# Moving a square root from ScalarE to VectorE at the entry of an attention backward pass, with spaced stores of q and a projection by whole tiles

## The chip, the cores and the metric

One core of one Trainium2 chip. The metric is the time of one execution on the device in microseconds (us). Two programs are compared by their fast runs of the same rounds on the same chip; "the span" is what a profile of one execution shows from its first to its last instruction, some 2 us less than its time.

## The reference

The program computes the output and all gradients of two attentions over the same tokens, in bf16. Part A is a linear attention and ends before the parts that matter here; part B is a softmax attention with 16 query heads and one head for k and v:

```python
def _B_ref(x, wq, wk, wv, wo):          # x: 1 x 2048 x 448
    B, S, D = x.shape
    H = 16
    Dh = D // H                          # 28, padded to 32 in the kernel
    q = (x @ wq).reshape(B, S, H, Dh).transpose(0, 2, 1, 3)
    k = x @ wk
    v = x @ wv
    scores = jnp.einsum("bhqd,bkd->bhqk", q, k) * (Dh ** -0.5)
    p = softmax(scores, axis=-1)
    o = jnp.einsum("bhqk,bkd->bhqd", p, v)
    return o.transpose(0, 2, 1, 3).reshape(B, S, H * Dh) @ wo
# out = concat([a, b]); outputs: out and the vjp of out for all eight inputs
```

## The kernel before: the parts that the change touches

The kernel first runs part A and the gradients that need no softmax (some 190 us), then the entry of part B, then a core of 512 units that computes exponentials, their transposes (eN, by DMA) and the products for dq, dk, dv and o, then a tail of some 75 us. The softmax needs no maximum: each row of q gets a shift, the root of |q|² times the largest |k|², written into a spare row of q.

The entry. Four quarters of q (512 tokens each) are projected; each gives its shift, a 16x512 tile; after two quarters the half of q is transposed by DMA into the tile qn and stored to qn_d in DRAM.

```python
        for qc in range(NQC):                      # four quarters of q
            ...                                    # projection, squares, sums of squares into pn
            shift = shifts[qc]
            nc.scalar.activation(out=shift, in_=pn[0:H, :], func=ACT.Sqrt, scale=kmax2[:, 0:1])
            for g in range(4):
                nc.gpsimd.dma_start(qT[:, g, qs].rearrange("(j r) s -> j r s", r=32)[:, 0, :], shift[4 * g:4 * g + 4, :])
            if qc % 2:
                q2 = slice((qc - 1) * 512, (qc + 1) * 512)
                t2 = slice(4 * qc - 4, 4 * qc + 4)
                for g in range(4):
                    nc.sync.dma_start_transpose(qn[:, t2, g * P:(g + 1) * P], qT[:, g, q2])
                nc.sync.dma_start(qn_d[q2, :].rearrange("(t p) c -> p t c", p=P), qn[:, t2, :])
```

Here qn is gaB, a tile that shows as gaT in the profile. The core, from its first exponential on:

```python
        do_slots = {u: divmod(n, 2) for n, u in enumerate([*range(1, 16), *range(17, 27, 2), *range(32, 128, 8)])}
        with tc.manual_schedule():
            tc.keep_in_program_order(nc.scalar.activation(out=ex[:], in_=ex[:], func=ACT.Exp))   # loads the table of exp
            for u in range(NU + 28):
                ...
                dpj = do_slots.pop(u, None)        # half a token tile of do = grad_out @ wo^T
                if dpj is not None:
                    dps_ = DB[u % 2] if u < 16 else dk_acc if u < 27 else spare
                    do_proj(*dpj, dps_)
                if hasS:
                    nc.scalar.activation(out=eT(u)[:, 0, :], in_=sp[0][:, :], func=ACT.Exp, scale=scale)
                ...
                # loads of q by tokens, for dk: four pieces per 256 tokens
                for a in {10: (0,), 14: (2,), 18: (1,), 22: (3,)}.get(u, ()) or {34: (0,), 42: (2,), 50: (1,), 58: (3,)}.get(u % 64, ()) * (u < 448):
                    ...
                    nc.gpsimd.dma_start(qX[qc][32 * a:32 * a + 32, :, :, :]..., qn_d[qc * 256:(qc + 1) * 256, :]...)
```

## Time and profile before

| kernel before | |
|---|---|
| time, median of 3 runs | 1078.06 us (1077.77 to 1078.93) |
| span of the profiled execution | 1079.1 us (its time: 1080.88 us) |
| first exponential of the core | 220.51 us |
| core, units 0 to 127 | 202.4 us |
| core, unit 128 to the last exponential | 581.3 us |
| tail | 75.0 us |

The prediction below walks through the views. In them PE is TensorE and PEld its weight loads, DVE is VectorE, ACT ScalarE, POOL GpSimd, SPq the queue of SyncE; a line of a timeline gives start and length in us, engine, line of the kernel, operation, result<-operands, shapes, count, and in brackets how long the engine idled before and what ended that (the releaser). An eviction is the copy of a result out of PSUM. Here is the head of the page alone: busy time of each engine, and the clock of TensorE in 40 slices of 27 us, in tenths of full speed. The one dip, an 8 in the tenth slice (243 to 270 us), lies in units 16 to 31 of part B's core.

```profile
PE 1027.6 (95%) x16326; PEld 489.1 (45%) x16329; DVE 895.5 (83%) x1792; ACT 876.7 (81%) x1744; POOL 772.1 (72%) x1014
...
PEclk9999999998999999999999999999999999999999
```

To compare executions I count the entry from "k0", the last eviction that ScalarE does for the gradients ahead of part B's entry (191.3 us here):

```profile
191.25 0.54 ACT L516 ACTIVATE wdq<-agen 128x448 bf16<-128x448 f32 x1 [1.54 <-PE agen L81]
192.17 0.69 ACT L563 ACTIVATE R<-agen,neg 128x512 bf16<-128x512 f32 x1 [0.37 <-PE agen L81]
```

The first eviction of k (the second line) follows 0.9 us later. The expectations below call k0 "the first eviction of k" or "the first row of k"; their numbers are counted from the first line.

### The profile page before, as it was taken

Reading aid. Unit: us, or ns where it says so; the run is one execution under the profiler, and the core shown is the slowest. Engines: PE = TensorE matmul, PEld = TensorE weight load, DVE = VectorE, ACT = ScalarE, POOL = GpSimd, SP = SyncE. Lnnn points to the kernel's source line nnn. Section 1 sums busy time; section 2 is a strip of 40 time slices with the busy share of each in tenths; the row PEclk is TensorE's granted clock in tenths of the full one; section 3 lists DMA queues with packets and bytes.
Section 4 is the critical chain, followed back from the end, with each engine's and each line's share of the span. In section 5 each row is a group of like instructions: output and inputs, shape, how many; then the busy total and the mean of one; then the engine's idle time right before and its main releaser. Section 6 shows DMA issues by size and latency. Waiting matters only on the chain.

```text
span 1079.1 us, 40135 instructions
## 1 busy us (share of the span) xinstructions
PE 1027.6 (95%) x16326; PEld 489.1 (45%) x16329; DVE 895.5 (83%) x1792; ACT 876.7 (81%) x1744; POOL 772.1 (72%) x1014
## 2 busy tenths in 40 slices
PE   9999999998999999999999999999999999999998
PEld 5555455443444444444444444444444444444434
DVE  7897400447999999999999999999999999999943
ACT  6463122577999999999999999999999999999622
POOL 6001243327888888888988888988998899888881
PEclk9999999998999999999999999999999999999999
DMA  9979899499999999999999999999999999999973
GB/s 239 165 131 195 161 196 193 88 215 169 202 210 198 179 190 187 197 188 201 183 187 191 201 188 194 204 184 182 193 203 186 193 194 193 196 177 180 221 140 92
DMA packets 669026, 199.36 MB, mean 185 GB/s; under 512 B 646008, under 2 KB 664736, under 8 KB 668840
## 3 DMA queue, kind: packets, MB, share of 16 engines
q1 hardware_dynamic: 656296, 175.23, 95.5%
q0 software_dynamic: 7584, 17.59, 6.9%
q10 hardware_dynamic: 4960, 3.96, 1.4%
q8 instruction: 128, 2.10, 0.8%
q14 instruction: 58, 0.48, 0.2%
HBM read 20.99 MB, written 12.94 MB: 31 GB/s over the span
## 4 chain that ended last, share of the span: by engine, by line
PE 34%; POOL 18%; ACT 18%; DVE 14%; issue 12%; DMA 4%; DVEq 0%; ACTq 0%; POOLq 0%; SPq 0%
POOL dsT L912 13%; PE agen L81 13%; ACT cp L911 9%; ACT eT L944 7%; DVE dsx L975 6%; PE sps L653 5%; PE aacc L81 4%; PE oq L653 4%; DVE dsT L909 3%; DMA eN<-eT 2%; PE dv_acc L653 2%; POOL prod L800 1%; PE dps L653 1%; DMA out_dram<-dsT 1%; DVE R L929 1%
## 5 line engine op out<-in xcount | busy, mean ns | idle before, releaser
L912 POOL TENSOR_TENSOR dsT<-cp,eT 128x512 bf16<-128x512 bf16 x512 | 588.4, 1157 | 104.5 <-ACT cp L911 98.6
L975 DVE STREAM_TRANSPOSE dsx<-dsT 128x512 f32<-128x512 f32 x512 | 357.7, 699 | 2.3 <-DVE R L723 0.2
L653 PEld LDWEIGHTS <-R 128*32 128x32 bf16 (+1 forms) x9184 | 229.5, 94 | 278.8 <-issue 238.7
L909 DVE TENSOR_TENSOR dsT<-dps,eT 128x512 bf16<-128x512 f32 x512 | 341.6, 667 | 16.5 <-PE dps L653 11.7
L904 ACT ACTIVATE eT<-sps 128x512 bf16<-128x512 f32 x512 | 312.6, 611 | 22.9 <-PE dps L653 10.7
L911 ACT ACTIVATE cp<-dps 128x512 bf16<-128x512 f32 x512 | 314.2, 614 | 12.0 <-PE dps L653 10.9
L944 ACT ACTIVATE eT<-sps 128x512 bf16<-128x512 f32 x512 | 320.3, 626 | 0.0
L653 PE MATMUL dk_acc<-dsx,qX 32*32 32x512 bf16 x4096 | 268.3, 376 | 0.0
L653 PE MATMUL dps<-doT,R 32*128 32x256 bf16 x2048 | 248.7, 270 | 1.9 <-ACT cp L911 0.8
L653 PE MATMUL sps<-R,R 32*128 32x256 bf16 (+1 forms) x2240 | 222.1, 274 | 7.6 <-DVE R L879 1.7
L653 PE MATMUL oq<-eT,R 128*32 128x256 bf16 x2048 | 158.3, 275 | 1.4 <-issue 1.4
L653 PE MATMUL oq<-dsT,R 128*32 128x256 bf16 x2048 | 157.1, 275 | 0.1
L653 PEld LDWEIGHTS <-qX 32*32 32x32 bf16 x4096 | 79.8, 89 | 114.4 <-issue 54.1
L653 PE MATMUL dv_acc<-eN,don 128*32 128x512 bf16 x1024 | 98.1, 381 | 3.8 <-DMA eN<-eT 3.8
L81 PEld LDWEIGHTS <-R 128*128 128x128 bf16 (+1 forms) x525 | 41.5, 98 | 41.7 <-issue 12.2
L406 POOL COPY pk<-R 128x256 bf16<-128x256 bf16 x4 | 1.6, 399 | 73.2 <-DVE R L366 73.1
L653 PEld LDWEIGHTS <-don 128*32 128x32 bf16 x1024 | 33.8, 97 | 5.0 <-issue 4.5
L422 DVE TENSOR_TENSOR osb<-aacc,pr 64x448 bf16<-64x448 f32 x2 | 1.2, 616 | 41.1 <-ACT pr L421 24.9
L800 POOL TENSOR_TENSOR prod<-R,oTs 128x128 f32<-128x128 bf16 x64 | 28.0, 438 | 7.7 <-DVE oTs L796 7.4
L929 DVE TENSOR_SCALAR R<-oq 64x256 bf16<-64x256 f32 x64 | 27.3, 427 | 3.6 <-PE oq L653 1.6
L817 PE MATMUL sps<-identB,don 128*32 128x128 bf16 x256 | 18.6, 224 | 12.3 <-POOL don L809 8.4
L81 PE MATMUL agen<-R,R 128*128 128x448 bf16 x128 | 28.6, 352 | 0.0
(232 smaller groups left out, 978.7 us busy)
## 6 DMA issues: line engine op xcount, KB each, us to landing
qX<-qn_d POOLq DMA_DIRECT2D x32, 256.0 KB, 4.3
out_dram<-osb ACTq DMA_DIRECT2D x22, 112.0 KB
qn_d<-gaT SPq DMA_DIRECT2D x2, 1024.0 KB
eN<-eT SPq DMA_TRANSPOSE x128
xa<-in_A_x_dram SPq DMA_DIRECT2D x8, 224.0 KB
ga<-in_grad_out_dram SPq DMA_DIRECT2D x4, 448.0 KB
xa<-in_grad_out_dram POOLq DMA_DIRECT2D x4, 448.0 KB, 12.2
out_dram<-wdq POOLq DMA_DIRECT2D x8, 224.0 KB, 6.3
```

Of the source, the lines that this page charges most:

```text
L81: nc.tensor.matmul(out_ap, lhsT=lhsT, rhs=rhs, start=start, stop=stop, tile_position=(0, 0))
L406: nc.gpsimd.tensor_copy(out=pk[:, t4, D:512], in_=gqn[:, t4, 3 * P:D])
L653: nc.tensor.matmul(out, lhsT=lhsT, rhs=rhs, start=start, stop=stop, tile_position=pos, skip_group_check=True)
L800: nc.gpsimd.tensor_tensor(out=prod[b][:], in0=dnv, in1=os_, op=ALU.mult)
L817: nc.tensor.transpose(tp2[q:q + 32, qb * P:(qb + 1) * P], don[b][:, qb, h, :], identB[:, :], tile_position=(0, q))
L904: nc.scalar.activation(out=eT(u)[:, 0, :], in_=sp[0][:, :], func=ACT.Exp, scale=scale)
L909: nc.vector.tensor_tensor(out=dst[:, 0, :], in0=dp[0][:, :], in1=ew[:, 0, :], op=ALU.mult)
L911: nc.scalar.activation(out=cp[:, :], in_=dp[1][:, :], func=ACT.Copy)
L912: nc.gpsimd.tensor_tensor(out=dst[:, 1, :], in0=cp[:, :], in1=ew[:, 1, :], op=ALU.mult)
L929: nc.vector.tensor_scalar(out=qT_B[g][64 * hp:64 * hp + 64, qc * 256:(qc + 1) * 256], in0=oq[64:128, 0:256], scalar1=scale, scalar2=None, ...
L944: nc.scalar.activation(out=eT(u)[:, 1, :], in_=sp[1][:, :], func=ACT.Exp, scale=scale)
L975: nc.vector.transpose(out=dsx[b][:, tp, :, :, :].rearrange("p h t c -> p (h t c)").bitcast(F32), in_=dsT[y][:, :, :].rearrange("p h c -> p ...
```

## The change

Its intent is to have no table loads on ScalarE for the square root, to take the second half's store off the entry, and to project do in fewer and larger pieces. Cut to its core:

```diff
-        return xbT, wq_pad, rep, bsel, gaB, ga[:, 8:12, :]
+        return xbT, wq_pad, rep, bsel, xa[:, 0:8, :], ga[:, 8:12, :], [flat(gaB[:, 2 * i:2 * i + 2, :]).bitcast(F32) for i in range(3)]
...
-            shift = shifts[qc]
-            nc.scalar.activation(out=shift, in_=pn[0:H, :], func=ACT.Sqrt, scale=kmax2[:, 0:1])
...
-            if qc % 2:
...
-                    nc.sync.dma_start_transpose(qn[:, t2, g * P:(g + 1) * P], qT[:, g, q2])
-                nc.sync.dma_start(qn_d[q2, :].rearrange("(t p) c -> p t c", p=P), qn[:, t2, :])
+            if qc == NQC - 1:
+                break
+            q_shift(pn, shifts[qc], qs, tmp)
+            if qc == 1:
+                for g in range(4):
+                    nc.sync.dma_start_transpose(qn[:, :, g * P:(g + 1) * P], qT[:, g, 0:1024])
+                nc.sync.dma_start(qn_d[0:1024, :].rearrange("(t p) c -> p t c", p=P), qn)
...
+    def q_shift(pn, shift, qs, tmp):
+        a, y, r = (t[0:H, :] for t in tmp)
+        nc.scalar.activation(out=a, in_=pn[0:H, :], func=ACT.Identity, bias=eps[:, 0:1], scale=kmax2[:, 0:1])
+        nc.vector.tensor_scalar(out=y.bitcast(mybir.dt.int32), in0=a.bitcast(mybir.dt.int32), scalar1=1, scalar2=None,
+                                op0=ALU.logical_shift_right)
+        nc.vector.tensor_scalar(out=y, in0=y, scalar1=0.485 * 2.0 ** 63.5, scalar2=None, op0=ALU.mult)
+        nc.vector.reciprocal(out=r, in_=y)
+        nc.vector.tensor_tensor(out=r, in0=r, in1=a, op=ALU.mult)
+        nc.vector.scalar_tensor_tensor(out=shift, in0=r, scalar=0.25, in1=y, op0=ALU.mult, op1=ALU.add)
+        for g in range(4):
+            nc.gpsimd.dma_start(R1[:, g, qs]..., shift[4 * g:4 * g + 4, :])
...
-        do_slots = {u: divmod(n, 2) for n, u in enumerate([*range(1, 16), *range(17, 27, 2), *range(32, 128, 8)])}
+        do_slots = {2 * i + 1: (i, 0, 512) for i in range(13)}
+        do_slots.update({32 + 8 * n: (13 + n // 2, n % 2 * 256, n % 2 * 256 + 256) for n in range(6)})
         with tc.manual_schedule():
-            tc.keep_in_program_order(nc.scalar.activation(out=ex[:], in_=ex[:], func=ACT.Exp))
+            qn = pqb_.tile([P, 8, 512], BF16, name="qX")
+            for g in range(4):
+                nc.sync.dma_start_transpose(qn[:, :, g * P:(g + 1) * P], R1[:, g, 1024:2048])
...
+                if u == 1:
+                    q_shift(*last_shift, ...)
...
+                for n in {34: (0,), 42: (1,), 50: (2,), 58: (3,)}.get(u, ()):
+                    nc.gpsimd.dma_start(qn_d[1024 + 256 * n:1280 + 256 * n, :].rearrange("(t p) c -> p t c", p=P),
+                                        qn[:, 2 * n:2 * n + 2, :])
```

So the root becomes a halved exponent and one Newton step on VectorE, with three tiles of scratch in gaT; the first half of q moves from gaT to xa; the second half is transposed inside the core and stored in four pieces on GpSimd's queue; the last shift is computed in unit 1. Not shown in the cut: four loads of q move to units 66 to 78, the load of wo from unit 70 to 86, and the PSUM pools of the entry and the core become one.

More of the change, by code (lines that the diff above doesn't have):

```diff
@@ L76 @@
     make_identity(nc, identB[:])
-    ex = cst.tile([P, 1], F32, name="ex")
-    nc.vector.memset(ex[:], 0.0)
+    kmax2 = cst.tile([H, 1], F32, name="kmax2")
+    eps = cst.tile([H, 1], F32, name="eps")
+    nc.vector.memset(eps[:], 1e-30)
     def mm(out_ap, lhsT, rhs, start=True, stop=True):
@@ L525, in phase_A @@
             dma_T(v4(R2), xa, 4 * q4, 4)
-        return xbT, wq_pad, rep, bsel, gaB, ga[:, 8:12, :]
+        return xbT, wq_pad, rep, bsel, xa[:, 0:8, :], ga[:, 8:12, :], [flat(gaB[:, 2 * i:2 * i + 2, :]).bitcast(F32) for i in range(3)]
     def phase_B_pre(pa, cA, awk, psA, io):
-        xbT, wq_pad, rep, bsel, qn, sh = io
+        xbT, wq_pad, rep, bsel, qn, sh, tmp = io
         kT, vT, vaug, kn, qT = kT_rep, vT_rep, vaug_, kn_, R1
@@ L571, in phase_B_pre @@
         shifts = [flat(sh)[0:H, i * 512:(i + 1) * 512] for i in range(NQC - 1)] + [flat(R3)[0:H, 5120:5632]]
-        kmax2 = cA.tile([H, 1], F32, name="kmax2")
         for qc in range(NQC):
@@ L590, in phase_B_pre @@
                     mm(pn[:, :], bsel[:, g - 2, :], sqs[g - 2][:, :], start=(g == 2), stop=(g == 5))
-            shift = shifts[qc]
-            nc.scalar.activation(out=shift, in_=pn[0:H, :], func=ACT.Sqrt, scale=kmax2[:, 0:1])
-            for g in range(4):
-                nc.gpsimd.dma_start(qT[:, g, qs].rearrange("(j r) s -> j r s", r=32)[:, 0, :], shift[4 * g:4 * g + 4, :])
-            if qc % 2:
-                q2 = slice((qc - 1) * 512, (qc + 1) * 512)
-                t2 = slice(4 * qc - 4, 4 * qc + 4)
+            if qc == NQC - 1:
+                break
+            q_shift(pn, shifts[qc], qs, tmp)
+            if qc == 1:
                 for g in range(4):
-                    nc.sync.dma_start_transpose(qn[:, t2, g * P:(g + 1) * P], qT[:, g, q2])
-                nc.sync.dma_start(qn_d[q2, :].rearrange("(t p) c -> p t c", p=P), qn[:, t2, :])
+                    nc.sync.dma_start_transpose(qn[:, :, g * P:(g + 1) * P], qT[:, g, 0:1024])
+                nc.sync.dma_start(qn_d[0:1024, :].rearrange("(t p) c -> p t c", p=P), qn)
         for rows, dst in [(vT, vaug_), (kT, kn_)]:
@@ L606, in phase_B_pre @@
         nc.gpsimd.memset(vaug_[:, :, 0:1], 1.0)
+        return pn, shifts[NQC - 1], qs
+    def q_shift(pn, shift, qs, tmp):
[8 more added lines that the diff above has]
+        for g in range(4):
+            nc.gpsimd.dma_start(R1[:, g, qs].rearrange("(j r) s -> j r s", r=32)[:, 0, :], shift[4 * g:4 * g + 4, :])
     R3f = flat(R3)
@@ L611 @@
     kn_ = R3f[:, 4608:5120].rearrange("p (t c) -> p t c", c=32)
+    psc = ExitStack()
+    psA = psc.enter_context(tc.tile_pool(name="psA", bufs=4, space=bass.MemoryType.PSUM))
     with ExitStack() as pa:
-        psA = pa.enter_context(tc.tile_pool(name="psA", bufs=4, space=bass.MemoryType.PSUM))
         cA = pa.enter_context(tc.tile_pool(name="cA", bufs=1, side="right"))
@@ L617 @@
         io = phase_A(pa, cA, cB, awk, psA)
-        phase_B_pre(pa, cA, awk, psA, io)
+        last_shift = phase_B_pre(pa, cA, awk, psA, io)
     NB = 64
@@ L623 @@
     vaug, kn, do_nat = vaug_, kn_, R2x[:, 0:NS, :]
-    psc = ExitStack()
     with ExitStack() as cs_:
-        psA = psc.enter_context(tc.tile_pool(name="psAcc", bufs=1, space=bass.MemoryType.PSUM))
         pe_ = cs_.enter_context(tc.tile_pool(name="ceT", bufs=1, side="right"))
@@ L635 @@
         pp_ = cs_.enter_context(tc.tile_pool(name="cout", bufs=2, side="right"))
-        SB = [psA.tile([P, 512], F32, name=f"sps{i}") for i in range(3)]
-        DB = [psA.tile([P, 512], F32, name=f"dps{i}") for i in range(2)]
-        oq = psA.tile([P, 512], F32, name="oq")
-        dv_acc = psA.tile([P, 512], F32, name="dv_acc")
-        dk_acc = psA.tile([P, 512], F32, name="dk_acc")
+        SB = [psA.tile([P, 512], F32, name="aacc") for i in range(3)]
+        DB = [psA.tile([P, 512], F32, name="agen") for i in range(2)]
+        oq, dk_acc = (psA.tile([P, 512], F32, name="agen") for _ in range(2))
         dsT, dsx, qX, don, doT, rl, prod = ({} for _ in range(7))
@@ L859, in o_dq, with dv_mm @@
                         next(g_)
-        def dv_mm(b, h, qb):
+        def dv_mm(dv_acc, b, h, qb):
             for c in range(4):
@@ L866, in dv_mm, with do_proj, do_copy @@
                     b == 0 and h + qb == 0, b == NB - 1 and h + qb == 2)
-        def do_proj(i, h, ps):
-            if ps is DB[0] or ps is DB[1]:
-                for c in range(4):
-                    mm(ps[:, 0:256], gbT[:, i, c, :], woTp[:, c, h * 256:(h + 1) * 256], start=(c == 0), stop=(c == 3))
-                return
+        def do_proj(i, c0, c1, ps):
             for c in range(4):
+                if c1 - c0 == 512:
+                    mm(ps[:, :], gbT[:, i, c, :], woTp[:, c, :], start=(c == 0), stop=(c == 3))
+                    continue
                 for j in range(4):
                     js = slice(32 * j, 32 * j + 32)
-                    mmt(ps[js, 0:256], gbT[:, i, c, js], woTp[:, c, h * 256:(h + 1) * 256], (0, 32 * j), c == 0, c == 3)
-        def do_copy(i, h, ps):
-            nc.vector.tensor_copy(out=do_nat[:, i, h * 256:(h + 1) * 256], in_=ps[:, 0:256])
-        do_slots = {u: divmod(n, 2) for n, u in enumerate([*range(1, 16), *range(17, 27, 2), *range(32, 128, 8)])}
+                    mmt(ps[js, 0:c1 - c0], gbT[:, i, c, js], woTp[:, c, c0:c1], (0, 32 * j), c == 0, c == 3)
+        def do_copy(i, c0, c1, ps):
+            nc.vector.tensor_copy(out=do_nat[:, i, c0:c1], in_=ps[:, 0:c1 - c0])
+        do_slots = {2 * i + 1: (i, 0, 512) for i in range(13)}
+        do_slots.update({32 + 8 * n: (13 + n // 2, n % 2 * 256, n % 2 * 256 + 256) for n in range(6)})
         with tc.manual_schedule():
-            tc.keep_in_program_order(nc.scalar.activation(out=ex[:], in_=ex[:], func=ACT.Exp))
+            qn = pqb_.tile([P, 8, 512], BF16, name="qX")
+            for g in range(4):
+                nc.sync.dma_start_transpose(qn[:, :, g * P:(g + 1) * P], R1[:, g, 1024:2048])
             for u in range(NU + 28):
@@ L899 @@
                 if dpj is not None:
-                    dps_ = DB[u % 2] if u < 16 else dk_acc if u < 27 else spare
+                    dps_ = DB[u // 2 % 2] if u < 16 else dk_acc if u < 27 else spare
                     do_proj(*dpj, dps_)
@@ L904 @@
                     nc.scalar.activation(out=eT(u)[:, 0, :], in_=sp[0][:, :], func=ACT.Exp, scale=scale)
+                if u == 1:
+                    q_shift(*last_shift, [pd_.tile([P, 2, 512], BF16, name="dsT").rearrange("p a b -> p (a b)").bitcast(F32)
+                                          for _ in range(3)])
+                    dv_acc = psA.tile([P, 512], F32, name="aacc")
                 if hasD:
@@ L912 @@
                     nc.gpsimd.tensor_tensor(out=dst[:, 1, :], in0=cp[:, :], in1=ew[:, 1, :], op=ALU.mult)
-                for a in {10: (0,), 14: (2,), 18: (1,), 22: (3,)}.get(u, ()) or {34: (0,), 42: (2,), 50: (1,), 58: (3,)}.get(u % 64, ()) * (u < 448):
-                    qc = u // 64 + (u > 24)
+                for n in {34: (0,), 42: (1,), 50: (2,), 58: (3,)}.get(u, ()):
+                    nc.gpsimd.dma_start(qn_d[1024 + 256 * n:1280 + 256 * n, :].rearrange("(t p) c -> p t c", p=P),
+                                        qn[:, 2 * n:2 * n + 2, :])
+                for a in {10: (0,), 14: (2,), 18: (1,), 22: (3,), 66: (0,), 70: (2,), 74: (1,), 78: (3,)}.get(u, ()) or {
+                        34: (0,), 42: (2,), 50: (1,), 58: (3,)}.get(u % 64, ()) * (96 < u < 448):
+                    qc = u // 64 + (u > 96)
                     if a == 0:
@@ L918 @@
                                         qn_d[qc * 256:(qc + 1) * 256, :].rearrange("(b j s) c -> j b (s c)", b=4, s=2))
-                if u == 70:
+                if u == 86:
                     nc.gpsimd.dma_start(wo, wo_d[:, 0:D].rearrange("(g p) c -> p g c", p=P))
@@ L957 @@
                     for k in {0: (0, 1), 2: (2,), 6: (3,)}.get(n, ()) if 0 <= b < NB else ():
-                        dv_mm(b, k // 2, k % 2)
+                        dv_mm(dv_acc, b, k // 2, k % 2)
                 y = u - 18
```

## The prediction

> **What bounds the kernel now.** I read the table of stretches first, because the page averages stages with different limits. The lines are stretches of the kernel before: start and end, length, busy time with count for PE, PEld, DVE, ACT and POOL, then the granted clock, the DMA share and GB/s.
>
> ```profile
> 192.00:218.00 26.00, 25.74 (x138) 11.11 (x139) 13.61 (x30) 14.91 (x24) 9.53 (x17) 1.00 0.42 73
> 218.00:222.50 4.50, 2.34 (x23) 1.15 (x23) 1.57 (x3) 4.06 (x8) 2.85 (x7) 1.00 0.74 149
> 222.60:225.90 3.30, 3.30 (x22) 1.32 (x22) 0.47 (x2) 1.95 (x4) 0.00 (x0) 0.50 1.05 272
> 249.90:253.20 3.30, 3.23 (x38) 0.96 (x37) 1.32 (x3) 1.62 (x4) 1.74 (x3) 0.50 1.28 160
> 267.00:270.30 3.30, 3.30 (x48) 1.29 (x40) 2.30 (x5) 2.62 (x6) 1.17 (x2) 0.50 1.06 223
> 423.00:1004.00 581.00, 558.22 (x10968) 259.19 (x10960) 566.54 (x1099) 574.55 (x1152) 513.39 (x609) 1.00 1.13 191
> ```
>
> The attention core has 512 units. From 423 on ScalarE is busy 574.55 of 581 us, VectorE 566.54, TensorE 558.22: three engines are full, and the change touches none of that. It works at the entry: the projection of q (192 to 218, TensorE busy 25.74 of 26), the handover (218 to 222.5), and the first 128 units, with three stretches at half clock, each behind a stall. So nothing here is worth more than some ten us of 1078.
>
> Next, who holds the entry: ScalarE's timeline, SyncE's, and the chain of waits.
>
> ```profile
> 218.41 0.68 ACT L592 ACTIVATE R<-aacc,kmax 16x512 bf16<-16x512 f32 x1 [0.93 <-PE aacc L81]
> 219.10 1.28 ACT L883 ACT_TABLE_LOAD   x1
> 220.40 0.20 ACT L883 ACTIVATE ex<-ex 128x1 f32<-128x1 f32 x1
> 220.51 0.58 ACT L904 ACTIVATE eT<-sps 128x512 bf16<-128x512 f32 x1
> ```
> ```profile
> 212.47 5.94 SPq L599 DMA_TRANSPOSE gaT<-R  x4
> 220.64 0.36 SPq L600 DMA_DIRECT2D qn_d<-gaT  x1
> 221.16 8.80 SPq L599 DMA_TRANSPOSE gaT<-R  x4
> 230.07 5.32 SPq L946 DMA_TRANSPOSE eN<-eT  x1
> 235.55 0.46 SPq L600 DMA_DIRECT2D qn_d<-gaT  x1
> ```
> ```profile
> 216.51 3.62 DMA R<-ga
> 220.40 0.20 ACT ex L883
> 236.06 13.86 DMA eN<-eT
> 256.13 9.73 DMA eN<-eT
> ```
>
> The reader should see: the first exponential starts at 220.51 and is held by two things ending together, the table load (220.38) and the third shift's DMA (chain, to 220.14). SyncE transposes the first half of q at 212.47, stores it at 220.64 once those have landed, transposes the second half, and only then issues the first transpose of the exponentials (230.07, though unit 3 ended near 226); the second store (235.55) comes before the next. Twice the chain runs through an eN transpose: dv's first matmuls (units 20 and 28) stand still for it.
>
> Starts of a unit's first exponential give the pace. Units 0, 16, 32, 128: 220.51, 241.84, 272.41, 422.89. Units 0 to 15 cost 21.3 us, 16 to 31 cost 30.6, a full block of eight 12.0 to 12.2. Unit 20 takes 3.78 and unit 28 4.20 instead of 1.5.
>
> [...]two loads of 1283 ns here (204.10 and 219.10), and none for Identity at 192. [...]the nearest row, an fp32 stream transpose of 128x512, takes 699. [...]
>
> **The change part by part.**
>
> *Square root.* Removed: two table loads (2.57 us of ScalarE), four Sqrt, the dummy Exp. Added: four Identity (the same 0.68) and per shift five VectorE operations on 16x512 fp32. The tile has only 16 partitions, but the 16x512 reduce takes 672 ns, so length is what is paid. Estimate: two tensor_scalar at 0.42 ([...]as the bf16 product of 512 at 424 ns), and reciprocal, product and scalar_tensor_tensor at 0.69: 2.9 us per shift instead of 0.68. TensorE is full until 218, so the load at 204 gives almost nothing back.
>
> *Where the chain stands.* The built order of VectorE puts the second shift's five operations after all four squares of the third quarter of q and mixes them with the first two squares of the fourth. In the trace the last square of the third quarter ends at 213.4. Then 0.42+0.42+0.69, a square 0.42, 0.69, a square 0.42, 0.69: 3.75, so this shift is ready at 217.1; before it was ready at 210.48. Everything behind it moves: its DMA and the first transpose (212.47, 2.0 later) go to 219.1; the last landing and the store of the first half (220.64, 8.2 later) to 227.3.
>
> *The wait that takes the place of the table load.* The first half of q now lies in xa, not in gaT. In the built program the first exponential waits, beside the shift DMAs, for the four transposes into xa and for the store from xa to land: the exponentials' buffers lie where phase A's tiles were. Before, nothing of gaT was in its wait list. The store needs about 5 us (issued 220.64; GpSimd's first load that needs it was issued at 226.81). So the first exponential starts near 227.3+5 = 232.3, against 220.51: +11.8. This is my main step.
>
> *Units 0 to 15.* By the chain of waits two units cost TensorE twice 0.42 for S, two half projections at 0.54 and 0.54 for o: 2.46. A whole tile is 4 matmuls of 512 columns, 0.85 and about 0.1 for the switch, an estimate: 2.33. Eight pairs save 1.0. [...] About even: 21.3.
>
> *Units 16 to 31.* The exponentials start 12 us late while SyncE's queue has only the second half's transposes before them, and no second store. The second eN transpose should land near 250 and unit 20 starts near 259: no stall. This takes away 2.2 in block 16 and 3.7 in block 24 (14.46 and 16.12 against 12.3 to 12.4), half-clock times included: -5.9. Five odd units project a whole tile (0.95) instead of a half (0.55); a half in the full core costs 0.31 (blocks 96 to 127: 12.47 against 12.17 without; 64 to 95: 12.3 against 12.0), so +1.2.
>
> *Units 32 to 127.* Six half projections (80 to 120) go: 6 x 0.31 = -1.9. The second half's store now goes out in four pieces on GpSimd's queue at units 34 to 58, and the loads of q move to 66 to 78: the same bytes. Block 48 took 13.93 instead of 12.46 because of a 1.4 us gap on TensorE without a releaser; half of it, -0.7, may go.
>
> Sum: +11.8 +0.0 -5.9 +1.2 -1.9 -0.7 = +4.5: 1078.06 + 4.5 = 1082.5.
>
> **The rivals.** (a) The entry opens early: the table load is gone, so the first exponential starts near 219 (-1.6), and with -5.9 and -1.9 the kernel takes about 1070. For it: that is the intent, and the chain passes through the activation of ex. Against it: the wait list. (b) The late entry is paid in full and the stalls on eN stay, since DMA is over its full share at the entry (1.05 to 1.28) and the spaced stores meet the loads: 1078 + 11.8 - 1.9 = 1088. For it: the eN transpose of 236.06 took 10.5 us beside other transfers. Against it: exponentials that start late have their transfers started with less in front of them. (c) Nothing moves, because the late entry is just what the eN transposes would have cost anyway: 1078.
>
> **Range and chances.** (a) gets about one in eight, (b) one in six, the rest lies around my sum. 1082.5, with 1073 to 1088 to hold it eight times in ten. Two per cent is 21.6 us: no step comes near. Faster 0.01, same 0.97, slower 0.02.
>
> **What would show it.** No table load after 30 us in ScalarE's timeline; its first exponential near 232 with a long idle time before it, released by the store of q; the store near 227; no wait of dv on eN; blocks 80 to 127 at 12.0 to 12.2; from 128 on the same pace. A first exponential before 222, or a store before 222, would break the main step; a unit 20 of over 3 us would break the second.

The +0.0 of units 0 to 15 ("about even") was made of -1.0 for whole tiles, and +0.8 for more time at half clock, an estimate that rested on no measurement. Ahead of "The change part by part" two readings of the trace stay: the table loads on ScalarE (1283 ns each, none ahead of the Identity at 192), and the 699 ns of a stream transpose, which the author took as the row nearest to the root's operations. For the 0.69 us this profile also has 686 and 688 ns for casts of 512 fp32 elements a partition (L993 and L605, 32 and 128 partitions), 687 for a tensor_scalar (L998), 667 for a product (L909) and 672 for a reduce (L550). That a reciprocal takes as long was an estimate by length alone, and the 0.42 us of a tensor_scalar one from the 424 ns of the bf16 product.

## The result

| | before | after |
|---|---|---|
| time, median of 4 runs | 1078.49 us (1077.77 to 1079.88) | 1091.24 us (1089.79 to 1092.16) |
| ratio of fast runs, 95% interval | | 1.0115 (1.0098 to 1.0133) |
| span of the profiled execution (its time) | 1079.1 (1080.88) | 1088.7 (1090.39) |

A ratio is the mean time of one kernel's fast runs over that of the other's fast runs of the same rounds, so not quite the ratio of the medians. The change makes the kernel 1.15% slower, within the 2% called "same", but outside the range that I had given: I had +4.5 us, it is about +12.4 (0.0115 x 1078.5).

The head of the page of the kernel after:

```profile
PE 1026.0 (94%) x16145; PEld 484.1 (44%) x16145; DVE 913.3 (84%) x1799; ACT 874.2 (80%) x1741; POOL 773.9 (71%) x1018
...
PEclk9999999969999999999999999999999999999999
```

ScalarE lost 2.5 us and VectorE gained 17.8, though the change added twenty short VectorE instructions and removed thirteen evictions of do. The dip of the clock is a deep 6 in the ninth slice (218 to 245 us) now: the granted clock was 0.50 from 219.4 to 239.9 us, and TensorE stood still for 14.03 us of that, to 233.48. ScalarE's timeline at the entry says why: its last work of the entry, then the first exponential.

```profile
217.18 0.77 ACT L608 ACTIVATE gaT<-aacc,eps,kmax 16x512 f32<-16x512 f32 x1 [1.45 <-DVE gaT L613]
232.83 0.60 ACT L913 ACTIVATE eT<-aacc 128x512 bf16<-128x512 f32 x1 [14.89 <-DMA qn_d<-xa]
```

No table load is left there, and yet ScalarE idles 14.89 us, until the store of q from xa (qn_d<-xa) has landed. SyncE's timeline shows that store's history, to be held against the 212.47 and 220.64 of before:

```profile
220.27 5.53 SPq L596 DMA_TRANSPOSE xa<-R  x4
227.88 0.36 SPq L597 DMA_DIRECT2D qn_d<-xa  x1
228.41 7.03 SPq L892 DMA_TRANSPOSE qX<-R  x4
239.10 17.65 SPq L963 DMA_TRANSPOSE eN<-eT  x3
```

And VectorE's timeline shows what the transposes waited for, the second shift:

```profile
211.97 0.41 DVE L609 TENSOR_SCALAR gaT<-gaT 16x512 int32<-16x512 int32 x1
212.42 0.41 DVE L611 TENSOR_SCALAR gaT<-gaT 16x512 f32<-16x512 f32 x1
212.87 3.34 DVE L612 RECIPROCAL gaT<-gaT 16x512 f32<-16x512 f32 x1
...
216.41 0.67 DVE L613 TENSOR_TENSOR gaT<-gaT 16x512 f32<-16x512 f32 x1
...
217.34 0.67 DVE L614 SCALAR_TENSOR_TENSOR ga<-gaT 16x512 bf16<-16x512 f32 x1
```

Four of the five operations take what I had given them, to 0.02 us (0.41, 0.41, 0.67, 0.67). The reciprocal takes 3.34 us, not 0.69.

In the core, the longest waits of ScalarE and TensorE from 215 us on are the late entry itself; the wait of dv on the transposed exponentials, two times and 3.8 us before, is gone.

```profile
ACT eT L913 <- DMA qn_d<-xa: 14.9, 1, 14.9
PE aacc L660 <- ACT eT L913: 14.0, 1, 14.0
```
```profile
PE dv_acc L653 <- DMA eN<-eT: 3.8, 2, 2.4
```

(The first fence is the kernel after, the second the kernel before; the columns are us in total, times, longest.)

The starts of the units' first exponentials divide the spans into stages, which tell where the time came from:

| stage, us | before | after | difference | predicted |
|---|---|---|---|---|
| k0 to the first exponential | 29.2 | 43.3 | +14.1 | +11.8 |
| units 0 to 15 | 21.3 | 22.2 | +0.9 | 0 |
| units 16 to 31 | 30.6 | 26.4 | -4.2 | -4.7 |
| units 32 to 79 | 76.0 | 75.6 | -0.4 | -0.7 |
| units 80 to 127 | 74.5 | 72.6 | -1.9 | -1.9 |
| unit 128 to the last exponential | 581.3 | 583.6 | +2.3 | 0 |
| tail | 75.0 | 75.5 | +0.5 | 0 |
| sum | | | +11.3 | +4.5 |

(The work ahead of k0 was 1.8 us shorter in the profiled execution after than in that of before; it lies inside the scatter of this stage. So these two executions account for 11.3 of the 12.4 us.) The surplus of 2.3 after unit 128 lies in one place, the block of units 440 to 447: 14.9 us instead of 12.2. GpSimd's timeline there:

```profile
905.34 1.16 POOL L925 TENSOR_TENSOR dsT<-cp,eT 128x512 bf16<-128x512 bf16 x1 [0.31 <-ACT cp L924]
907.80 0.58 POOL L934 DMA_DIRECT2D qX<-qn_d  x1 [1.30 <-issue]
```

GpSimd idles 1.30 us ahead of the issue of a load of q, and the trace shows no event that it waits for. Before has no such gap in the core.

### The profile page after: what moved, and what is told of

Read it like the earlier page. It is cut to its first block, busy times and chain, and to the rows that moved or that the text cites. A ratio compares the mean times of both kernels' runs of the same rounds, so it can differ in the third digit from the quotient of the medians.

```text
span 1088.7 us, 39768 instructions
## 1 busy us (share of the span) xinstructions
PE 1026.0 (94%) x16145; PEld 484.1 (44%) x16145; DVE 913.3 (84%) x1799; ACT 874.2 (80%) x1741; POOL 773.9 (71%) x1018
## 4 chain that ended last, share of the span: by engine, by line
PE 36%; ACT 20%; POOL 20%; DVE 11%; issue 11%; DMA 2%; SPq 0%; ACTq 0%; DVEq 0%; POOLq 0%
POOL dsT L925 15%; PE agen L82 13%; ACT cp L924 10%; ACT eT L961 8%; PE agen L660 7%; PE aacc L82 7%; PE aacc L660 7%; DVE dsx L992 3%; DVE dsT L922 2%; POOL prod L807 1%; POOL don L810 1%; ACT eT L913 1%; PE aacc L824 1%; POOL R L811 1%; DVE oTs L943 1%
## 5 line engine op out<-in xcount | busy, mean ns | idle before, releaser
L660 PEld LDWEIGHTS <-R 32*128 32x128 bf16 (+1 forms) x9008 | 224.7, 94 | 294.4 <-issue 257.2
L922 DVE TENSOR_TENSOR dsT<-agen,eT 128x512 bf16<-128x512 f32 x512 | 341.4, 667 | 12.9 <-PE agen L660 8.2
L913 ACT ACTIVATE eT<-aacc 128x512 bf16<-128x512 f32 x512 | 313.1, 612 | 33.8 <-DMA qn_d<-xa 14.9
L924 ACT ACTIVATE cp<-agen 128x512 bf16<-128x512 f32 x512 | 315.3, 616 | 12.3 <-PE agen L660 11.2
L961 ACT ACTIVATE eT<-aacc 128x512 bf16<-128x512 f32 x512 | 321.7, 628 | 0.0
L660 PE MATMUL agen<-dsx,qX 32*32 32x512 bf16 x4096 | 268.6, 377 | 0.0
L660 PE MATMUL agen<-doT,R 32*128 32x256 bf16 x2048 | 248.7, 269 | 4.5 <-DVE dsT L922 1.8
L660 PE MATMUL aacc<-R,R 32*128 32x256 bf16 (+1 forms) x2144 | 219.5, 274 | 19.6 <-ACT eT L913 14.0
L660 PE MATMUL agen<-eT,R 128*32 128x256 bf16 x2048 | 157.8, 275 | 0.0
L660 PE MATMUL agen<-dsT,R 128*32 128x256 bf16 x2048 | 156.8, 275 | 0.1
L660 PE MATMUL aacc<-eN,don 128*32 128x512 bf16 x1024 | 97.0, 380 | 0.0
L423 DVE TENSOR_TENSOR osb<-aacc,pr 64x448 bf16<-64x448 f32 x2 | 1.2, 617 | 38.1 <-DMA out_dram<-osb 24.1
L824 PE MATMUL aacc<-identB,don 128*32 128x128 bf16 x256 | 18.5, 223 | 14.1 <-POOL don L816 10.2
```

Of the source, the lines that this page charges most:

```text
L660: nc.tensor.matmul(out, lhsT=lhsT, rhs=rhs, start=start, stop=stop, tile_position=pos, skip_group_check=True)
L824: nc.tensor.transpose(tp2[q:q + 32, qb * P:(qb + 1) * P], don[b][:, qb, h, :], identB[:, :], tile_position=(0, q))
L922: nc.vector.tensor_tensor(out=dst[:, 0, :], in0=dp[0][:, :], in1=ew[:, 0, :], op=ALU.mult)
L924: nc.scalar.activation(out=cp[:, :], in_=dp[1][:, :], func=ACT.Copy)
L961: nc.scalar.activation(out=eT(u)[:, 1, :], in_=sp[1][:, :], func=ACT.Exp, scale=scale)
```

## The experiments

Four questions: is it the store from xa that holds the first exponential; is it the reciprocal that makes that store late; where does block 440 come from; and is there a version that keeps what the change wins. In the kernel before, the runs of the three batches had medians of 1080.5, 1079.93 and 1082.93 us (11 runs each, 1075.67 to 1088.51 over all), so each ratio is taken within its batch, over six runs of the experiment. Every result was correct.

### The store from xa alone: xa_only

The kernel before, with only the first half of q going through xa. Roots, do and loads stay.

```diff
-        return xbT, wq_pad, rep, bsel, gaB, ga[:, 8:12, :]
+        return xbT, wq_pad, rep, bsel, [xa[:, 0:8, :], gaB[:, 8:16, :]], ga[:, 8:12, :]
...
-                    nc.sync.dma_start_transpose(qn[:, t2, g * P:(g + 1) * P], qT[:, g, q2])
-                nc.sync.dma_start(qn_d[q2, :].rearrange("(t p) c -> p t c", p=P), qn[:, t2, :])
+                    nc.sync.dma_start_transpose(qn[qc // 2][:, :, g * P:(g + 1) * P], qT[:, g, q2])
+                nc.sync.dma_start(qn_d[q2, :].rearrange("(t p) c -> p t c", p=P), qn[qc // 2])
```

> The kernel before with one edit: the first half of q is transposed into xa and stored from there, instead of gaT; root on ScalarE, stores and do as before. Account 1 (the first exponential must wait for that store, because the exponentials' buffers lie where xa lay): the store is issued near 220.6 and lands near 225.8 as before, so the first exponential starts near 226 instead of 220.5, released by the store; with the stalls on eN partly absorbing it, the kernel is 2 to 5 us slower. Rival (the lateness is made by VectorE's root alone, the place of q does not matter): first exponential at 220.5, time unchanged within 1 us.

Measured: 1084.18 us (1081.36 to 1085.09), ratio 1.0027 (0.9999 to 1.0055). The first exponential starts at k0+35.1 instead of k0+29.2. SyncE's and then ScalarE's timeline:

```profile
214.76 5.80 SPq L599 DMA_TRANSPOSE xa<-R  x4
223.12 0.36 SPq L600 DMA_DIRECT2D qn_d<-xa  x1
```
```profile
221.38 1.28 ACT L883 ACT_TABLE_LOAD   x1
222.67 0.20 ACT L883 ACTIVATE ex<-ex 128x1 f32<-128x1 f32 x1
228.67 0.60 ACT L904 ACTIVATE eT<-sps 128x512 bf16<-128x512 f32 x1 [5.79 <-DMA R<-R]
```

With the table loaded at 222.7 the first exponential waits another 5.8 us. The line names a shift's DMA (R<-R), but that is not what held it. The trace also records the steps of ScalarE's own queue that wait for semaphores. The wait for the store's semaphore passes at 228.13, those behind it 0.08 us apart until 228.59, and the named DMA landed only at 228.38, in between. The store was issued at 223.12 and its last packet ended at 227.7. So the store held it, and the move of half of q to another buffer costs the entry 5.9 us by itself. The whole kernel is 2.9 us slower by the ratio, with an interval that reaches 1. Units 16 to 31 take 24.4 us instead of 30.6, as if the late entry were given back there; but four_more, below, has the same 24.4 us without a late entry, so this is not shown.

### The first half back in gaT: gat_back

The kernel after, with the first half of q in gaT again and the root's scratch behind it.

```diff
-        return ..., xa[:, 0:8, :], ga[:, 8:12, :], [flat(gaB[:, 2 * i:2 * i + 2, :]).bitcast(F32) for i in range(3)]
+        return ..., gaB[:, 0:8, :], ga[:, 8:12, :], [flat(gaB[:, 8 + 2 * i:10 + 2 * i, :]).bitcast(F32) for i in range(3)]
```

> The changed kernel with one edit: the first half of q back in the first half of gaT, the root's scratch in the rest of gaT. Account 1: the store is no longer in the wait list of the first exponential, but the DMAs of the third shift are, whose root ends at 225.1 in the changed kernel; they land near 229, so the first exponential starts near 229 instead of 232.8. The second half's transposes now wait for the store instead (their buffer lies over gaT), so eN starts later and may stall dv again: kernel 0 to 4 us faster than the changed one, 9 to 12.5 us slower than before. Rival (the place of q is the whole of it): first exponential near 221, kernel within 3 us of before.

Measured: 1088.26 us (1086.08 to 1089.66), ratio 1.007 (1.0043 to 1.0098). ScalarE:

```profile
229.32 0.60 ACT L913 ACTIVATE eT<-aacc 128x512 bf16<-128x512 f32 x1 [11.23 <-DMA R<-ga]
```

The first exponential starts at k0+39.7, no longer released by the store but by the DMA of the third shift (R<-ga), which is just as late because of the root. So the buffer is worth 3.6 us in the changed kernel, and 10.5 us of the entry's delay against before remain. The store is still issued late, at 227.85. Block 440 is as slow as in the kernel after (14.95), so the buffer has nothing to do with that. The whole was better than expected: 7.6 us slower than before by the ratio, where I had 9 to 12.5.

### The projection of do alone: do_only

The kernel before, with the changed do_proj, do_copy and do_slots.

```diff
-        do_slots = {u: divmod(n, 2) for n, u in enumerate([*range(1, 16), *range(17, 27, 2), *range(32, 128, 8)])}
+        do_slots = {2 * i + 1: (i, 0, 512) for i in range(13)}
+        do_slots.update({32 + 8 * n: (13 + n // 2, n % 2 * 256, n % 2 * 256 + 256) for n in range(6)})
...
-                    dps_ = DB[u % 2] if u < 16 else dk_acc if u < 27 else spare
+                    dps_ = DB[u // 2 % 2] if u < 16 else dk_acc if u < 27 else spare
```

> The kernel before with only the new do projection (whole tiles in odd units to 25, six halves to unit 72). From blocks 80 to 127 of the changed kernel (72.6 against 74.5 us) 1.9 us faster there; units 16 to 31 about 1.2 slower; units 0 to 15 about 1 faster by less TensorE work: kernel 1 to 2.5 us faster than before. If whole tiles in the odd units cost as much as they save, it is within 0.5 us of before.

Measured: 1079.37 us (1073.95 to 1082.76), ratio 0.9984 (0.9949 to 1.0019). In the profile units 80 to 127 take 72.6 us, as in the kernel after, against 74.5. The 1.9 us that I had predicted for this part are there, but the whole time scatters by 9 us and does not settle a gain of 0.2%. The rest of the expectation failed in this execution: units 0 to 15 took 25.4 us, not 1 us less than the 21.3 of before, at a mean granted clock of 0.68 (0.92 in before); and units 16 to 31 took 26.8 us, not 1.2 more than 30.6, with no wait on eN.

### The root by two operations: two_ops

The kernel after, with the Newton step left out: the shift is 0.97 of the rough root times its constant, still a usable shift.

```diff
-        nc.vector.tensor_scalar(out=y, in0=y, scalar1=0.485 * 2.0 ** 63.5, scalar2=None, op0=ALU.mult)
-        nc.vector.reciprocal(out=r, in_=y)
-        nc.vector.tensor_tensor(out=r, in0=r, in1=a, op=ALU.mult)
-        nc.vector.scalar_tensor_tensor(out=shift, in0=r, scalar=0.25, in1=y, op0=ALU.mult, op1=ALU.add)
+        nc.vector.tensor_scalar(out=shift, in0=y, scalar1=0.97 * 2.0 ** 63.5, scalar2=None, op0=ALU.mult)
```

> The changed kernel with the root cut to its first two VectorE operations (the reciprocal, product and last sum gone; the shift is then some per cent off, which the row sums cancel). Account 1 with the reciprocal as the mis-sized term (3.33 us measured against 0.69 estimated): the second shift is ready near 210 instead of 218, its store is issued near 220 and lands near 225; the first exponential starts near 225, still released by the store: kernel 6 to 9 us faster than the changed one. Rival (the reciprocal is hidden, only the order behind the squares counts): no more than 2 us faster.

Measured: 1082.27 us (1080.85 to 1083.58), ratio 1.0016 (0.9989 to 1.0043). ScalarE:

```profile
227.59 0.60 ACT L910 ACTIVATE eT<-aacc 128x512 bf16<-128x512 f32 x1 [9.20 <-DMA qn_d<-xa]
```

Still released by the store from xa, but at k0+35.9, 7.4 us earlier: nearly where xa_only has it. By the ratios it is 10.7 us faster than the kernel after, more than the 6 to 9 that I had expected. So the entry's delay has two parts, the buffer and the length of the root. The scheduler also placed the second shift ahead of the third quarter's squares here, so this run cannot say which operation counts.

### The reciprocal alone: short_recip

The kernel after, with the reciprocal replaced by a product with 0 of the same tile, so that all five operations stay. (The constant 0.97 keeps the shift near the root.)

```diff
-        nc.vector.tensor_scalar(out=y, in0=y, scalar1=0.485 * 2.0 ** 63.5, scalar2=None, op0=ALU.mult)
-        nc.vector.reciprocal(out=r, in_=y)
+        nc.vector.tensor_scalar(out=y, in0=y, scalar1=0.97 * 2.0 ** 63.5, scalar2=None, op0=ALU.mult)
+        nc.vector.tensor_scalar(out=r, in0=y, scalar1=0.0, scalar2=None, op0=ALU.mult)
```

> The changed kernel with the reciprocal of the root replaced by a multiplication by 0 of the same tile, and the first constant 0.97 instead of 0.485, so that the other four VectorE operations stay and the shift is still about the root (within some 3 per cent). The reciprocal of 16x512 took 3.34 us, a tensor_scalar of the same tile 0.41: each root gets 2.9 us shorter. Theory (the reciprocal is what my prediction of the entry missed): the first exponential starts, counted from the first eviction of k, 2.9 us earlier than in the changed kernel if only the second shift's own reciprocal is on the path, 5.9 if the first shift's is too: 43.3 becomes 37.4 to 40.4; the ratio to the kernel before 1.0035 to 1.009 (the changed kernel: 1.0115). Rival (the length of five dependent operations and their waits, not the reciprocal): 43.3 within 1 us and 1.0115. Block 440 stays slow, since the stores stay on GpSimd's queue.

Measured: 1088.75 us (1085.0 to 1091.14), ratio 1.0049 (1.0019 to 1.0078). The first exponential starts at k0+38.1, 5.2 us earlier than in the kernel after. VectorE's timeline, the second shift's first, third and last operation:

```profile
209.75 0.42 DVE L609 TENSOR_SCALAR gaT<-gaT 16x512 int32<-16x512 int32 x1 [0.32 <-ACT gaT L608]
...
210.88 0.41 DVE L612 TENSOR_SCALAR gaT<-gaT 16x512 f32<-16x512 f32 x1
...
212.25 0.68 DVE L614 SCALAR_TENSOR_TENSOR ga<-gaT 16x512 bf16<-16x512 f32 x1
```

Counted from k0 (190.1 here, 189.5 after), the second shift begins 2.9 us earlier and takes 3.2 us from its first operation to its last end, not 6.0. So two reciprocals lie on the path, that of the first shift and that of the second: the 5.2 us are near the 5.9 that I had expected for two, not the 2.9 for one. (Here too the order of instructions changes somewhat; the durations do not.) Block 440 stays at 14.95. The profile also has a stall of some 4 us at unit 27, where the first products of dk wait for a load of q; it is taken up below.

### Four transfers on GpSimd's queue: sp_stores and four_more

Two runs ask after block 440 from both sides. In sp_stores the kernel after issues its four spaced stores from SyncE; in four_more the kernel before gets four useless stores of the same size on GpSimd's queue in the same units.

```diff
# sp_stores, to the kernel after
-                    nc.gpsimd.dma_start(qn_d[1024 + 256 * n:1280 + 256 * n, :]...
+                    nc.sync.dma_start(qn_d[1024 + 256 * n:1280 + 256 * n, :]...
# four_more, to the kernel before
+                if u in (34, 42, 50, 58):
+                    nc.gpsimd.dma_start(dum_d[:, :].rearrange("(t p) c -> p t c", p=P),
+                                        R3f[:, 2048:3072].rearrange("p (t c) -> p t c", c=512))
```

> The changed kernel with the four spaced stores of q issued by SyncE instead of GpSimd; all else the same. In the changed kernel and in two variants of it block 440 (units 440 to 447) takes 13.5 to 14.95 us instead of 12.2, where GpSimd's load of q at 442 stands 1.3 us without a releaser; kernels without spaced stores on GpSimd's queue have no such block. If the four additional transfers on GpSimd's queue carry it (my account), block 440 takes 12.2 here and the kernel is 2 to 3 us faster than the changed one; first exponential unchanged near 43 us after the first row of k. Rival (the shifted code or the later entry does it): block 440 stays at 13.5 or more.

> The kernel before with four additional stores on GpSimd's queue at units 34 to 58, of the size and shape of the spaced stores, to a scratch that nobody reads; nothing else. If the count of transfers on that queue makes the slow block, block 440 takes 13.5 to 15 us here too and the kernel is 2 to 4 us slower than before; if not, 12.2 and under 1.5 us slower.

Measured: sp_stores 1086.61 us (1086.11 to 1095.25), ratio 1.0087 (1.0053 to 1.012); four_more 1088.18 us (1080.97 to 1092.85), ratio 1.0089 (1.0059 to 1.0119). With the stores on SyncE the slow block is gone: unit 128 to the last exponential takes 581.0 us. In the kernel before with four more stores it appears: blocks 440 and 448 take 13.51 and 13.03 us, and GpSimd shows the same gap ahead of an issue:

```profile
899.40 0.58 POOL L918 DMA_DIRECT2D qX<-qn_d  x1 [1.29 <-issue]
```

So four more transfers on GpSimd's queue at units 34 to 58 make a stall some 400 units later. By what mechanism, no run shows; before itself has gaps of 0.68 and 1.57 us ahead of issues of this queue at 1031.8 and 1037.25, past the core, and it is only a guess that these are the same hold at another place. A count from the traces fits that guess. In all five kernels with four more transfers on this queue the gap (1.29 to 1.30 us) stands ahead of the 99th DMA that GpSimd issues, when 6176 packets of its queue have moved. In the other eight kernels 6176 packets have moved only past the core, ahead of the 101st, where the gap is 0.07 to 0.69 us, and ahead of the 108th all eight have one of 1.57 to 1.59 us. So in these thirteen traces the gaps go with the count of the queue's traffic; what is counted there stays open. In four_more this explains only part of a ratio worth some 9.6 us: the profiled execution was the fastest of its six runs (1080.97 us), and shows 1.9 us past unit 128 and 2.3 us in units 32 to 79. What the slower ones lost stays open. The profile is also a second look at the kernel before, whose program it is up to unit 33. There units 0 to 15 took 23.7 us at a mean granted clock of 0.78 (21.3 at 0.92 in the profile of before) and units 16 to 31 took 24.4 (30.6), with no wait of dv on eN. So the stalls on eN do not come in every execution of the kernel before.

sp_stores had two runs of six near 1094 us, the profiled one among them. There the first dk stood 4.6 us for a load of q: the last of the four loads took 11.9 us to land (269.2 to 281.1), against 6.6 in the profile of the kernel after. So the SyncE stores are better by the four good runs, near 1086.4, but with a second stall that comes in some executions.

### Versions to beat both: two_gat_sp, exact_gat_sp

Both combine gat_back and sp_stores with the changed do. In two_gat_sp the root is that of two_ops. In exact_gat_sp it is Sqrt on ScalarE again for all four shifts, the last one ahead of the core; the dummy Exp stays out.

> The changed kernel with three edits: root cut to two VectorE operations, first half of q back in gaT, spaced stores issued by SyncE. By my account nothing late is left in the first exponential's wait list: the third shift's DMAs land about 27 us after the first row of k, so it starts 28 to 29.5 us after it (43.3 in the changed kernel, 29.2 before); units 0 to 127 take about 196 us as in the changed kernel, block 440 12.2: 5 to 9 us faster than before, 17 to 21 faster than the changed one. Rival (the second half's transposes, which must then wait for the store, delay the first eN so that dv stalls at units 20 and 28 again): no more than 2 us faster than before.

> As the former run but with Sqrt on ScalarE again, for all four shifts, and so with both table loads and no VectorE root: what the other parts of the change are worth alone. First exponential 29 to 30.5 us after the first row of k, units 0 to 127 about 196 to 198 us: 4 to 7 us faster than before, 0.5 to 2.5 us slower than with the short root.

Measured: two_gat_sp 1078.84 us (1075.88 to 1089.0), ratio 1.0007 (0.9969 to 1.0045); exact_gat_sp 1081.23 us (1074.15 to 1082.13), ratio 0.9996 (0.9964 to 1.0028). Neither gain shows, though the first exponential starts at k0+30.8 and k0+30.3, little behind the 29.2 of before. The runs of exact_gat_sp fall in two groups: 1074.15 and 1074.38, and four from 1081.04 to 1082.13. The profiled one belongs to the slow group, and its waits from 240 us on name the cause:

```profile
PEld L653 <- DMA qX<-qn_d: 5.3, 1, 5.3
PE agen L653 <- DMA qX<-qn_d: 5.0, 1, 5.0
```

The first products of dk wait for the last load of q: issued at 254.6, landed at 266.8, so 12.2 us instead of the 5.4 that the same load took in the kernel before. Units 16 to 31 cost 33.7 us instead of 26.4. This is the stall of sp_stores and short_recip again.

### The loads of q earlier: exact_early, two_early

The same two, with the first four loads of q moved up by four to seven units.

```diff
-                for a in {10: (0,), 14: (2,), 18: (1,), 22: (3,), 66: ...
+                for a in {6: (0,), 9: (2,), 12: (1,), 15: (3,), 66: ...
```

> A version to beat both: Sqrt on ScalarE for all four shifts, first half of q in gaT, second half's stores on SyncE in four pieces, projection of do by whole tiles, and the four first loads of q at units 6, 9, 12, 15 instead of 10, 14, 18, 22. In the same version without the last edit the first dk waited 5 us for the last of those loads (landed 266.8) in some executions and the runs fell in two groups of 1074 and 1081 us. If that wait makes the two groups: units 16 to 31 cost 26 to 27 us, not 33.7, in the profile, and the times lie at 1073 to 1076: ratio 0.994 to 0.996. If the loads only collide with other transfers earlier (the first transposes of the exponentials, the transposes of the second half of q): units 0 to 31 give back what is gained, ratio 0.998 to 1.002, with two groups still.

> The same with the root cut to two VectorE operations instead of Sqrt on ScalarE (no table load). Without the early loads its runs spread from 1076 to 1089. If the wait for the last load of q makes the spread: 1074 to 1077, ratio 0.994 to 0.997, within 0.002 of the version with Sqrt, since the first exponential started at k0+30.8 and k0+30.3 in those two. If not: spread over 5 us as before and a ratio of 0.998 to 1.002.

Measured: exact_early 1076.18 us (1073.4 to 1078.07), ratio 0.9934 (0.9906 to 0.9962); two_early 1082.44 us (1077.78 to 1085.46), ratio 0.9978 (0.9947 to 1.001).

exact_early is faster than the kernel before: all its six runs lie below all eleven of before's (1078.36 to 1086.8). Units 16 to 31 take 26.4 us and no run near 1081 is left, which is what the wait for q as the cause of the two groups led to expect (the version without early loads ran in another batch, on another chip, so the two are compared through before alone); the median is a little higher than I had expected, as before's is in this batch. SyncE's timeline, and the clock on its page:

```profile
211.44 5.65 SPq L596 DMA_TRANSPOSE gaT<-R  x4
219.74 0.36 SPq L597 DMA_DIRECT2D qn_d<-gaT  x1
```
```profile
PEclk9999999989999999999999999999999999999999
```

The transposes begin at 211.44, as early as in the kernel before, and the clock's dip is as shallow as there, not the 6 of the kernel after.

two_early is a miss: I had expected it within 0.002 of exact_early. Its first exponential starts at k0+30.8 and the wait for q is gone, but its profile, the slowest of the six runs (1085.46 us), has gaps of 2.7 and 2.5 us on TensorE at 361 and 499 us to which the trace gives no releaser. (Of the two gaps of two_gat_sp, the 2.5 us at 366 is a wait of dv on eN and the 2.3 us at 414 has no releaser.) What makes these gaps, and why the version with Sqrt was spared in its profiled executions, I cannot say.

## Why the prediction was wrong, point by point

**The main step, its mechanism: right.** I had said that the first exponential would wait for the store of the first half of q from xa. The line of ScalarE's timeline names that store, xa_only makes the wait in the kernel before, and gat_back takes it away.

**The main step, its size: wrong, in the term of the reciprocal.** The step put "reciprocal, product and scalar_tensor_tensor at 0.69". The other two took 0.67, the reciprocal 3.34. short_recip shows that two of them are on the path and cost 5.2 us of the entry. The error in the sum is only 2.3 us (+14.1 for +11.8) because another term erred the other way: I let the second shift start after the third quarter's last square, 22.1 us after k0. With the long reciprocals it starts 22.5 us after k0, but with short ones it was 19.6 (short_recip). The profile of before had what was needed. Its groups of VectorE by shape have two reciprocals, of 4 and of 64 elements a partition:

```profile
L320 DVE RECIPROCAL rden<-rden 128x64 f32<-128x64 f32 x4 | 2.2, 550 | 0.1
...
L795 DVE RECIPROCAL rl<-sps 128x4 f32<-128x4 f32 x64 | 10.1, 158 | 0.7 <-ACT eT L904 0.6
```

(550 - 158) / 60 is 6.5 ns per element; 448 elements more than 64 then make 0.55 + 2.9, or 3.5 us (measured in the kernel after: 3.334, so 6.2 ns for each of the 448). I had taken the row of a stream transpose as the "nearest", which it is in shape and not in operation.

**Units 0 to 15: right within 0.9 us.** I had counted -1.0 for whole tiles and +0.8, an estimate, for more time at half clock; 22.2 came for 21.3. In the profile of before the granted clock was 0.50 for 3.4 us of this stage (222.6 to 226.0), in that of after for 7.1 us (232.8 to 239.9), TensorE being back at work from 233.48 on. What this cost in us was not told apart from the gain of the tiles, and being this near is partly luck: over the profiles this stage takes from 20.8 to 25.4 us, and in those where I read the clock it is longer where the granted clock is lower (before 0.92, after 0.84, four_more 0.78, do_only 0.68: 21.3, 22.2, 23.7 and 25.4 us). What brings the half clock, no run shows. The length of a gap on TensorE alone does not decide: in the profile of before the clock was 0.50 at the end of a gap of 1.35 us (at 249.97) and again from 266.95, 1.0 us after the end of one of 2.41 us, but stayed at 1.00 after one of 1.41 us (ended at 299.84).

**Units 16 to 31: right in number, the reason not shown.** -4.2 for -4.7, and the wait of dv on the transposed exponentials left the list of waits, as the step said. But the step took the stalls in the profile of before for a fixed cost that only a late entry removes. four_more, the same program there, has none of them, and do_only, whose entry is as early as before's, has none either. Units 0 to 31 together took 51.9 us in the profile of before, 48.1 in four_more and 48.6 in the kernel after. So the -4.2 may be the scatter of one execution.

**Units 32 to 127: right.** -2.3 for -2.6, and do_only shows the -1.9 of units 80 to 127 by themselves.

**"The same bytes": wrong.** This step let the four stores and the moved loads stand for no cost past unit 128. Block 440 costs +2.7, and sp_stores and four_more show that it comes from the four transfers added to GpSimd's queue, not from their bytes.

**The rivals.** (a), an early entry near 219, fell with the wait list. (b), 1088, was nearest in time but for another reason: it had the stalls on eN stay, and they are not in the profile after. The sum from k0 is +11.3: my +4.5, plus 2.3 for the entry, 2.3 past unit 128, 0.9 in units 0 to 15, and 1.3 over the other stages.

**The range.** 1088 as its upper end left 5.5 us for a mis-sized term on the one path that sets the entry. Every estimate in that chain was counted once, while the shift's root stood on it twice.

What stays open: the mechanism of GpSimd's gap, how often the kernel before stalls on eN (it has one trace), the rest of four_more's loss, the gaps without releaser in two_early and two_gat_sp, and the loads of q that take 12 us in some executions and 6 in others.

## What to carry to other kernels

Price each operation on a row of the same operation, and take two lengths to get the cost per element; a reciprocal is not priced by a transpose or a product of the same length (here 3.33 us against 0.70 and 0.67). When a tile moves to another buffer, read which later tiles lie on that buffer, because their first writer then waits for the last reader of the old one (in xa_only the first exponential started 5.9 us later for that). And transfers added to a queue can stall it far from where they were added (here four stores on GpSimd's queue at units 34 to 58 brought a gap of 1.3 us at unit 442), so compare the whole core block by block, not only the stretch that was edited. A stall in one profile need not be in the next of the same program: before a gain is booked on removing it, look at a second profile.
